# One of four head pairs of the first batch moved from TensorE transposes in float32 to DMA transposes of float16 halves

## The chip, the cores and the metric

The kernel runs on one core of one Trainium2 chip. The metric is the time of one execution on the device in microseconds (us). Three runs of the kernel before lie between 962.21 and 963.56 us, with a median of 963.2 us.

## The reference, cut to what matters

Two batches of attention with 8 heads, 768 tokens and head size 64 are followed by two dense stages on all 1536 tokens. A query sees only the keys of its own cluster.

```python
def _attn_ref(q, k, v, centroids):
    # q_assign, k_assign: argmax over 16 clusters of the normalized products
    mask = q_assign[:, :, :, None] == k_assign[:, :, None, :]
    scores = scale * np.matmul(q, k.transpose(0, 1, 3, 2))
    scores = np.where(mask, scores, -1000000000.0)
    scores = scores - np.max(scores, axis=-1, keepdims=True)
    attn = np.exp(scores)
    attn = attn / (np.sum(attn, axis=-1, keepdims=True) + 1e-09)
    return np.matmul(attn, v).astype(np.float32)

def _moe_ref(x, w_in, w_out):            # 512 -> 2048 -> 512
    h = x @ w_in
    g = h * np.clip(h + 3.0, 0.0, 6.0) / 6.0
    return (g @ w_out).astype(np.float32)

def _moe2_ref(x, domain_probs, w1, w2):  # 4 experts, 512 -> 1024 -> 512
    p = domain_probs / (domain_probs.sum(-1, keepdims=True) + 1e-09)
    for e in range(4):
        out += p[:, e:e + 1] * (np.maximum(x @ w1[e], 0.0) @ w2[e])
    return out.astype(np.float32)
```

The dense stages run as products of float16 halves: a number is a high half plus a low half, and three of the four products are taken.

## The kernel before, in words

**Stages.** The attention of batch 0 comes first (some 150 us), then the dense stages of batch 0, into which the attention of batch 1 is woven, then the dense stages of batch 1.

**Attention.** Two heads make a pair, and there are four pairs. Three blocks of 256 queries make a pair's work, and each block has four units: two heads, 128 queries each. A unit is: the scores in PSUM by TensorE (`scores`, tile `pss`), the row maximum by VectorE (tile `ut`), the exponential by ScalarE (tile `e`, 128x768 float32), and two tiny VectorE steps that make the reciprocal of the row sum.

**Batch 0, `turned`.** GpSimd multiplies `e` by the reciprocal in place (L751). TensorE turns `e` in six 128x128 transposes of float32 (L763, tile `pst`, two halves of three). ScalarE (L770) or VectorE (L772) copies each half of 384 columns out of PSUM into `pt`; a list of five letters gives four of five copies to ScalarE. A block ends with twelve float32 products with the values (L779, tile `psv`), and ScalarE and VectorE split the sum into the halves `x1h` and `x1l` (L787, L788).

**Batch 1, `block`.** A unit's `e` becomes two float16 halves in the tile `p`: the high half by GpSimd or ScalarE, which multiply on the way (L873, L871), the low half by VectorE from `e` and the high half (L875). One DMA from SP's queue turns the whole tile (L812, 12 squares of 128x128). A block ends with 36 float16 products (L825), with the values in halves too (`vh`, `vl`, L733 and L734).

**Fillers.** The first dense stage's weights come as 64-bit numbers and are packed into float32 during the attention of batch 0 (`conv_w`). A step is one GpSimd row (L974) and three VectorE rows (L976, L978, L980) on 128x512. Four rows L902 and L899 split the weights into halves. When the x1 of all pairs for the first 384 tokens is there, TensorE starts on the first dense product (L993 to L995, tile `psg1`), four tiles of 12 products one after the other in one PSUM buffer, until the attention's PSUM buffers are given back.

**What sets the order.** Every instruction is recorded as a task with a priority, and `Order.plan` places them by a list scheduler with a table of costs: an engine takes the task that can start first, ties by priority. Tasks of GpSimd, and VectorE tasks marked `lk`, are never planned at the same time. The plan is fixed when the program is built; each engine then works through its own list in that order. The list `seq` gives the order of the twelve blocks of batch 0 (block 3*pair + i), and the numbers in `PAR` shift priorities.

Of the kernel before, what the change touches and what calls it, by code (L numbers as in the profile page):

```python
# [9 lines left out]
F32 = mybir.dt.float32  # L10
# [17 lines left out]
def _f32(u):  # L28
# [10 lines left out]
PAR = dict(  # L39
    thr=3060,  # L40
    off=0.0,
    wsl="DD",
    wx=-1.7848102153653658,
    wxs=1.64249681070015,
    wx0=43.52497423987616,
    wl=7.46084025153843,
    slack=0.05,
    nl=0.5,
    vre=2,
    nbv=12.87796141218993,  # L50
    nbr=18.542111538044182,
    xw=[4.0, 8.0],
    prl=60.0,
    q0=-100.0,
    q1=6.0,
    psc="ms",
    ql=6,
    ahead=2.5,
    wait=0,
    wait0=0.8,  # L60
    until=20.0,
    wgap=4,
    ta=33.746613078702275,
    tu=2.609752841226513,
    lead0=24.331100661201216,
    lead2=1.5253475332630761,
    vlead2=-8.583792241787163,
    lead1=2.038891508477018,
    vlead=-37.093258968816514,
    avp=-9.334810999175945,  # L70
    parts=3,
    avpa=-4.3000394462166165,
    kn='PPPPPD',
    kt='AAADA',
    kb='AAPD',
    gl=["DDDD", "DDDD"],
    mx=28.649235830032236,
    sp=15.01076876764054,
    spc=7.053784887436649,
    wse=dict(i="P", o="S", **{"1": "P", "2": "A"}),  # L80
    v0=42.0,
    lr=0.3,
    spm=1.5,
    pem=0.0,
    v1=-24.49398218583093,
    a_pool=dict(raw=2, vr=4, sc=1, so=1, cs=2, oh=3, sm=2, e=7, pt=5, tiny=11, stk=4),
    b_pool=dict(raw=2, vr=2, sc=1, so=1, cs=1, oh=1, sm=2, e=2, p=3, pt=3, vh=1, vl=1, tiny=11, stk=2),
    xbb=1,
    loa="VP",
    lob="VV",  # L90
    r64p=8.97904547225396,
    slow=1.1760075282760927,
    psx=3,
    dup=["PSSS", "P"],
# [17 lines left out]
    btail=7.42405243741263,
    bu0=40.446540415353034,
    bdu=26.208100345557234,
    bvl=-0.8085585893733991,
    bpr=6.32743258604082,
)


# [267 lines left out]
def body(ctx: ExitStack, tc: tile.TileContext, qk, vd, cent, w_in, w_out, probs, w1, w2, out):  # L387
    nc = tc.nc
    B, H, _, S = qk.shape
    D, C = 64, 16  # L390
    NP = H // 2
    NT = S // 128
# [15 lines left out]
    G = PAR  # L408
# [87 lines left out]
    wx = fixed([128, B, NC2, 2], F32, "wx")  # L496
# [10 lines left out]
    pt = fixed([128, NTOK // 128, E], F32, "pt")  # L507
    sp = fixed([128, NTOK // 128], F32, "sp")
# [65 lines left out]
    class Attn:  # L574
        def __init__(self, b, g, gp, n):
            self.b = b
            self.xb = PAR["xbb"]
# [146 lines left out]
        def values(self, hp, p):  # L724
            b, st = self.b, self.pair[hp]
            vr, inv, k = st["vr"], vm[:, b, 1:2], (vm, (b, 1))
            if b == 0:
                st["v"] = vr
                return
            vr = self.buf("vr", [128, 2, NT, D], F32)  # L730
            dma(393e3, max(p(0), self.seen + 0.1 * hp), lambda: nc.sync.dma_start(out=vr.t, in_=vd[b, hp]), [], [vr])
            vh, vl = self.buf("vh", [128, 2, NT, D], F16), self.buf("vl", [128, 2, NT, D], F16)
            act(S, p(2), lambda: nc.scalar.activation(out=vh.t, in_=vr.t, func=AF.Copy, scale=inv), [vr, k], [vh], ap=True)  # L733
            dve(S, p(2), lambda: nc.vector.scalar_tensor_tensor(  # L734
                out=vl.t, in0=vr.t, scalar=inv, in1=vh.t, op0=ALU.mult, op1=ALU.subtract), [vr, k, vh], [vl], ap=True, lk=True)
            st["v"] = (vh, vl)
# [54 lines left out]
        def block(self, hp, blk, p, kinds, xb, avp):  # L791

            b, st = self.b, self.pair[hp]
# [616 lines left out]
```

## Time and profile before

| | |
|---|---|
| Median of three runs | 963.2 us |
| The profiled execution | 964.7 us, span 962.9 us |
| Mean granted clock of TensorE | 0.993 of full speed |
| Busy, share of the span | PE 96%, DVE 76%, ACT 68%, POOL 37% |

Busy time is how long at least one instruction of the engine ran. PE is TensorE, DVE is VectorE, ACT is ScalarE, POOL is GpSimd and SP is the engine whose queue issues the DMAs. The shares are means over stages with different limits, so the change is read from the stage in which it lies: the attention of batch 0, from the first scores at about 13 us to the last of its blocks at about 148 us.

### The profile page before, as it was taken

The numbers are of one execution on the slowest core, as the hardware profiler recorded it, in microseconds if no ns is written. First come the engines' busy times: TensorE is split into PE (matmuls) and PEld (weight loads), VectorE is DVE, ScalarE is ACT, GpSimd is POOL, SyncE is SP. The second block draws the span as 40 slices with busy tenths as digits, with TensorE's granted clock in tenths as the row PEclk, the third lists the DMA queues.
The fourth block names the chain that finished last, engine by engine and source line by source line (L and its number), as shares of the span: only waits on it lengthen the run. The fifth ranks groups of instructions, "written<-read, shape, count | busy, mean of one in ns | idle before, by whom it ended". The sixth has DMA issues, their size and how long they took to land.

```text
span 962.9 us, 16168 instructions
## 1 busy us (share of the span) xinstructions
PE 922.3 (96%) x5633; PEld 546.9 (57%) x5633; DVE 727.3 (76%) x1513; ACT 658.4 (68%) x1372; POOL 356.8 (37%) x394
## 2 busy tenths in 40 slices
PE   5899999999989999999999999999999999999998
PEld 3577775555655565555565555666655555555553
DVE  8898785887779898799788986965578665554543
ACT  6899996767687796988788754566458654555411
POOL 3465744234533435736355321001132442434100
PEclk9999999999999999999999999999999999999999
DMA  7534339786526484586457587432021221212001
GB/s 235 142 89 116 127 106 328 237 288 206 175 93 188 90 174 104 127 179 132 120 107 182 152 159 191 144 109 90 21 67 66 88 70 63 88 45 87 1 1 66
DMA packets 124369, 121.63 MB, mean 126 GB/s; under 512 B 81472, under 2 KB 81472, under 8 KB 124288
## 3 DMA queue, kind: packets, MB, share of 16 engines
q1 hardware_dynamic: 124288, 120.61, 44.3%
q8 instruction: 44, 0.72, 0.3%
q14 instruction: 37, 0.30, 0.1%
HBM read 81.32 MB, written 14.68 MB: 100 GB/s over the span
## 4 chain that ended last, share of the span: by engine, by line
PE 44%; DVE 4%; ACT 3%; DMA 1%; POOL 1%; issue 1%; SPq 1%; POOLq 0%; ACTq 0%
PE psm L993 6%; PE psm L994 6%; PE psm L995 6%; PE psw L1070 6%; PE psw L1072 5%; PE psw L1071 5%; PE psg L995 2%; PE psg L993 2%; PE psg L994 2%; DMA wraw<-in_w 1%; PE psv L825 1%; PE pss L843 1%; ACT e L852 1%; PE pss L845 1%; DMA pt<-p 1%
## 5 line engine op out<-in xcount | busy, mean ns | idle before, releaser
L899 POOL TENSOR_TENSOR w<-wraw,w 128x512 f16<-128x512 f32 (+1 forms) x128 | 135.1, 1075 | 174.5 <-ACT w L898 132.1
L993 PE MATMUL psm<-w,h 128*128 128x512 f16 x384 | 146.3, 381 | 2.6 <-DVE h L1233 2.5
L995 PE MATMUL psm<-w,h 128*128 128x512 f16 x384 | 146.0, 380 | 0.1
L994 PE MATMUL psm<-w,h 128*128 128x512 f16 x384 | 146.0, 380 | 0.0
L851 DVE TENSOR_REDUCE ut<-pss 128x1 f32<-128x768 f32 x96 | 91.0, 951 | 16.8 <-PE pss L845 15.8
L852 ACT ACTIVATE e<-pss,ut 128x768 f32<-128x768 f32 x96 | 86.1, 898 | 18.0 <-DVE ut L851 15.3
L897 POOL TENSOR_SCALAR wraw<-wraw,wsc 128x512 f32<-128x512 f32 x64 | 45.8, 724 | 124.0 <-DMA wraw<-in_w 43.0
L1080 ACT ACTIVATE keep<-psw 128x384 f32<-128x384 f32 x96 | 46.7, 486 | 63.9 <-PE psw L1072 63.8
L898 ACT ACTIVATE w<-wraw 128x512 f16<-128x512 f32 (+1 forms) x128 | 72.4, 582 | 20.2 <-POOL wraw L897 11.1
L994 PE MATMUL psg<-g,w 128*128 128x384 f16 x256 | 83.4, 326 | 1.2 <-DVE g L1143 1.2
L993 PE MATMUL psg<-g,w 128*128 128x384 f16 x256 | 83.6, 327 | 1.0 <-DVE t L1141 0.6
L995 PE MATMUL psg<-g,w 128*128 128x384 f16 x256 | 83.6, 326 | 0.0
L1257 DVE SCALAR_TENSOR_TENSOR oa<-psm,pq,oa 128x512 f32<-128x512 f32 x84 | 61.9, 745 | 23.1 <-PE psm L995 23.1
L994 PEld LDWEIGHTS <-w 128*128 128x128 f16 x512 | 50.3, 98 | 39.0 <-issue 8.1
L995 PEld LDWEIGHTS <-w 128*128 128x128 f16 x512 | 50.2, 98 | 35.9 <-issue 3.3
L993 PEld LDWEIGHTS <-w 128*128 128x128 f16 x512 | 50.9, 99 | 33.4 <-issue 1.7
L843 PE MATMUL pss<-ka,qa 128*128 128x384 f32 x192 | 60.8, 398 | 8.1 <-ACT e L852 7.7
L1233 DVE SCALAR_TENSOR_TENSOR h<-psw,h 128x384 f16<-128x384 f32 x78 | 43.1, 553 | 29.0 <-ACT h L1232 28.8
L995 PEld LDWEIGHTS <-h 128*128 128x128 f16 x384 | 37.7, 98 | 46.1 <-DVE h L1233 0.6
L1070 PE MATMUL psw<-tx,ws 128*128 128x384 f16 x192 | 62.7, 327 | 0.9 <-ACT keep L1080 0.7
L1071 PE MATMUL psw<-tx,ws 128*128 128x384 f16 x192 | 62.6, 326 | 0.3 <-DVE tx L1022 0.3
L993 PEld LDWEIGHTS <-h 128*128 128x128 f16 x384 | 38.5, 100 | 42.5 <-issue 5.4
(199 smaller groups left out, 2402.6 us busy)
## 6 DMA issues: line engine op xcount, KB each, us to landing
wraw<-in_w SPq DMA_DIRECT2D x128, 256.0 KB, 3.4
r<-in_w_in SPq DMA_DIRECT2D x16, 512.0 KB, 4.6
r<-in_w_out SPq DMA_DIRECT2D x16, 512.0 KB, 3.9
w<-hl_i SPq DMA_DIRECT2D x32, 256.0 KB, 3.2
w<-hl_o SPq DMA_DIRECT2D x32, 256.0 KB, 3.9
raw<-in_qk SPq DMA_DIRECT2D x16, 384.0 KB, 4.3
vr<-in_vd SPq DMA_DIRECT2D x12, 384.0 KB, 4.9
hl_i<-w SPq DMA_DIRECT2D x16, 256.0 KB, 3.0
```

What stands on the lines that cost most here:

```text
L843: nc.tensor.matmul(ps[:, f, 0:HS], qa[:, qs], ka[:, f * HS:f * HS + HS], start=True, stop=False)
L851: dve(S, p, lambda: nc.vector.tensor_reduce(out=nb(), in_=ps[:, :, 0:HS], axis=AX.XY, op=ALU.max, negate=True), [ps], [(tb, n)])
L852: act(S, p, lambda: nc.scalar.activation(out=e.t.rearrange("p (a b) -> p a b", a=2), in_=ps[:, :, 0:HS], func=AF.Exp, bias=nb(), scale=1.0 ...
L898: act(c, p, lambda w=w, raw=raw, c=c: nc.scalar.activation(out=w[:, 0, 0:c], in_=raw[:, 0:c], func=AF.Copy), [raw], [(w, 0)])
L899: pool(c, p, lambda w=w, raw=raw, c=c: nc.gpsimd.tensor_tensor(out=w[:, 1, 0:c], in0=raw[:, 0:c], in1=w[:, 0, 0:c], op=ALU.subtract), [raw ...
L993: nc.tensor.matmul(o_, ah, bh, start=i == 0, stop=False)
L994: nc.tensor.matmul(o_, ah, bl, start=False, stop=False)
L995: nc.tensor.matmul(o_, al, bh, start=False, stop=i == 3)
L1070: nc.tensor.matmul(o_, ah, bh, start=not more and k == 0, stop=False, skip_group_check=more)
L1071: nc.tensor.matmul(o_, ah, bl, start=False, stop=False, skip_group_check=more)
L1072: nc.tensor.matmul(o_, al, bh, start=False, stop=k == 1, skip_group_check=more)
L1257: dve(512, p, lambda: nc.vector.scalar_tensor_tensor(out=oa[:, t], in0=ps.t, scalar=q, in1=oa[:, t], op0=ALU.mult, op1=ALU.add), [ps, qk], ...
```

## The change

Pair 2 of batch 0 (`ct0=(2,)`) goes through `block` in place of `turned`, with the letters `DDDD`: GpSimd makes the high half of each unit, VectorE the low half. The pair's values are split into `vh` and `vl` once. The blocks of pair 2 (6, 7, 8) alternate with those of pair 3 (9, 10, 11) in `seq`; before they stood 6, 7, 9, 10, 8, 11. Three tiles `p` and one each of `vh` and `vl` are added to batch 0's buffers. Many priorities in `PAR` have new values.

```diff
+    ct0=(2,),
+    kc="DDDD",
+    avc=-5.0,
+    vc=0.0,
...
-    seq=[0, 1, 3, 2, 5, 4, 6, 7, 9, 10, 8, 11],
+    seq=[0, 1, 3, 2, 5, 4, 9, 6, 10, 7, 11, 8],
...
-            if b == 0:
+            if b == 0 and hp not in G["ct0"]:
                 st["v"] = vr
                 return
-            vr = self.buf("vr", [128, 2, NT, D], F32)
-            dma(393e3, max(p(0), self.seen + 0.1 * hp), lambda: nc.sync.dma_start(out=vr.t, in_=vd[b, hp]), [], [vr])
+            if b:
+                vr = self.buf("vr", [128, 2, NT, D], F32)
+                dma(393e3, max(p(0), self.seen + 0.1 * hp), lambda: nc.sync.dma_start(out=vr.t, in_=vd[b, hp]), [], [vr])
...
-            col = XSC / (VSC * PSC)
+            col = XSC / (VSC * PSC) if b else 1.0 / PSC
...
         for blk in range(NBQ):
-            a0.turned(hp, blk, lambda i, t0=when[hp, blk]: t0 + i * T_UNIT, G["avpa"])
+            if hp in G["ct0"]:
+                a0.block(hp, blk, lambda i, t0=when[hp, blk]: t0 + i * T_UNIT, G["kc"], 1, G["avc"])
+            else:
+                a0.turned(hp, blk, lambda i, t0=when[hp, blk]: t0 + i * T_UNIT, G["avpa"])
```

In the changed kernel the same lines stand 4 or 5 lines further down (L763 is L768, L875 is L880, L978 is L983).

The first place is VectorE's list near the end of the attention of batch 0. `ut` is the row maximum or its tiny steps, `wconv` the weights that are packed, `pt` a turned half, `t` and `g` the first dense product's result, `x1l` a finished block. Before:

```order
L851 TENSOR_REDUCE ut_1869<-pss_1850 128x1
L772 COPY pt_1844<-pst_1865 128x384
L860 TENSOR_SCALAR ut_1831<-ut_1831 128x1
L980 SCALAR_TENSOR_TENSOR wconv_1669<-r64_1299,wconv_1669 128x512
L861 RECIPROCAL ut_1831<-ut_1831 128x1
L860 TENSOR_SCALAR ut_1869<-ut_1869 128x1
L978 SCALAR_TENSOR_TENSOR wconv_1823<-r64_1774,wconv_1823 128x512
L861 RECIPROCAL ut_1869<-ut_1869 128x1
L980 SCALAR_TENSOR_TENSOR wconv_1823<-r64_1774,wconv_1823 128x512
L1141 SCALAR_TENSOR_TENSOR t_1908<-t_1908,psg1_1835 128x384
L772 COPY pt_1894<-pst_1925 128x384
L788 SCALAR_TENSOR_TENSOR x1l0_611<-psv_1891,vm_66,x1h0_594 128x256
```

And now, at the same place (`p` is the tile of halves, L880 the low half):

```order
L983 SCALAR_TENSOR_TENSOR wconv_1887<-r64_1836,wconv_1887 128x512
L880 SCALAR_TENSOR_TENSOR p_1928<-e_1900,ut_1878,p_1928 128x768
L793 SCALAR_TENSOR_TENSOR x1l0_619<-psv_1909,vm_66,x1h0_611 128x256
L856 TENSOR_REDUCE ut_1962<-pss_1939 128x1
L880 SCALAR_TENSOR_TENSOR p_1956<-e_1907,ut_1893,p_1956 128x768
L865 TENSOR_SCALAR ut_1962<-ut_1962 128x1
L1148 TENSOR_TENSOR g_1937<-t_1916,g_1937 128x384
L866 RECIPROCAL ut_1962<-ut_1962 128x1
L1146 SCALAR_TENSOR_TENSOR t_1971<-t_1971,psg1_1948 128x384
L985 SCALAR_TENSOR_TENSOR wconv_1887<-r64_1836,wconv_1887 128x512
L880 SCALAR_TENSOR_TENSOR p_1979<-e_1968,ut_1962,p_1979 128x768
L1148 TENSOR_TENSOR g_1981<-t_1971,g_1981 128x384
```

The steps of the packing stand among the attention's steps as before; the copies out of PSUM have gone for pair 2, and a low half stands there for each of its units, the last one (p_1979) four rows ahead of the end of the attention's own work.

The second place is the end of TensorE's share of that attention: the last scores (`pss`), what stands between, and the last products with the values (`psv`). Before:

```order
L843 MATMUL pss_1850<-ka_1096,qa_1089 128x384 x2
L845 MATMUL pss_1850<-kb_1162,qb_1120 128x384 x2
L763 MATMUL pst_1859<-ident_60,e_1772 128x128 x3
L763 MATMUL pst_1865<-ident_60,e_1772 128x128 x3
...
L995 MATMUL psg1_1990<-x1h0_594,w_1593 128x384
L779 MATMUL psv_2009<-pt_1894,vr_316 64x256
```

And now:

```order
L848 MATMUL pss_1939<-ka_1182,qa_1168 128x384 x2
L850 MATMUL pss_1939<-kb_1191,qb_1188 128x384 x2
L998 LDWEIGHTS w_1429
L998 MATMUL psg1_1948<-x1h0_611,w_1429 128x384
...
L1000 MATMUL psg1_2010<-x1h0_611,w_1464 128x384
L830 LDWEIGHTS vh_567
L830 MATMUL psv_2020<-pt_1881,vh_567 64x256
```

Between the last scores and the last products with the values there now stand 30 products of the first dense stage (two and a half tiles `psg1`) and no transposes; 12 products of it stand ahead of the last scores and 6 behind the products with the values. Before, 33 of those 48 stood ahead of the last products with the values and 15 behind.

The third place is SP's list. Where loads of 64-bit weights (`r64`) stood one after the other, the DMA transposes now stand among them:

```order
L817 DMA_TRANSPOSE pt_1627<-p_1579 128x12x128
L975 DMA r64_1653<-in_w_in 128x1024
L817 DMA_TRANSPOSE pt_1627<-p_1638 128x12x128
L975 DMA r64_1704<-in_w_out 128x1024
L817 DMA_TRANSPOSE pt_1710<-p_1684 128x12x128
L817 DMA_TRANSPOSE pt_1710<-p_1708 128x12x128
L975 DMA r64_1757<-in_w_out 128x1024
```

Twelve transposes are added; a load behind one is issued only after the transpose has been, and that waits for its low half.

## Rows read from the trace of the kernel before

**Rows 1.** Busy time by stretch: from:to, us; PE, PEld, DVE, ACT, POOL; clock, DMA

```profile
13.00:80.00 67.00, 58.53 (x397) 42.94 (x394) 61.97 (x136) 59.23 (x124) 34.26 (x37) 0.95 0.50 141
80.00:148.60 68.60, 64.27 (x473) 49.33 (x473) 55.62 (x137) 61.45 (x140) 41.10 (x47) 1.00 0.38 119
153.00:300.00 147.00, 141.63 (x853) 83.05 (x851) 111.91 (x226) 109.61 (x228) 61.22 (x74) 0.99 0.64 217
```

**Rows 2.** Timeline of VectorE: start us, us, then the instruction; sixth block's end

```profile
79.91 0.48 DVE L788 SCALAR_TENSOR_TENSOR x1l<-psv,vm,x1h 128x256 f16<-128x256 f32 x1
```

**Rows 3.** Timeline of TensorE: a block's products with the values, a unit's transposes

```profile
46.01 2.81 PE L779 MATMUL psv<-pt,vr 128*64 128x256 f32 x24
48.75 0.88 PE L763 MATMUL pst<-ident,e 128*128 128x128 f32 x6
...
50.16 0.82 PE L763 MATMUL pst<-ident,e 128*128 128x128 f32 x6
50.74 0.60 PE L843 MATMUL pss<-ka,qa 128*128 128x384 f32 x2
```

**Rows 4.** Timeline of TensorE: a block of batch 1 and what follows it

```profile
335.92 0.85 PE L825 MATMUL psv<-pt,vh 128*64 128x256 f16 x12
...
338.01 0.39 PE L993 MATMUL psm<-w,h 128*128 128x512 f16 x1
```

**Rows 5.** Groups of instructions by form, 80 to 148.6 us: count, busy us, mean ns, idle

```profile
L751 POOL TENSOR_SCALAR e<-e,ut 128x768 f32<-128x768 f32 x26 | 23.9, 926 | 19.6 <-PE pst L763 6.7 <-DVE ut L861 3.8 <-ACT e L852 2.9
...
L770 ACT ACTIVATE pt<-pst 128x384 f32<-128x384 f32 x44 | 20.1, 494 | 1.7 <-PE pst L763 1.3
...
L772 DVE COPY pt<-pst 128x384 f32<-128x384 f32 x11 | 6.1, 551 | 2.5 <-PE pst L763 2.5
L978 DVE SCALAR_TENSOR_TENSOR wconv<-r,wconv 128x512 int32<-128x512 int32 x8 | 5.7, 715 | 0.1
...
L980 DVE SCALAR_TENSOR_TENSOR wconv<-r,wconv 128x512 int32<-128x512 int32 x8 | 5.5, 684 | 0.0
...
L976 DVE TENSOR_SCALAR wconv<-wconv 128x512 int32<-128x512 int32 x7 | 3.1, 444 | 0.8 <-POOL wconv L974 0.8
...
L902 DVE SCALAR_TENSOR_TENSOR w<-wconv,wsc,w 128x512 f16<-128x512 f32 x4 | 2.9, 745 | 0.0
...
L1143 DVE TENSOR_TENSOR g<-t,g 128x384 f16<-128x384 f32 x2 | 1.1, 550 | 0.0
...
L675 DVE TENSOR_TENSOR oh<-cs,mx 128x384 bf16<-128x384 f32 x1 | 0.9, 924 | 0.0
```

**Rows 6.** Instructions on tile p in batch 1: duration ns min/median/max; DMA landing

```profile
L875 DVE SCALAR_TENSOR_TENSOR p<-e,ut,p x36: 1000/1011/1602, 317.3 to 590.2; 128x768 f16<-128x768 f32 x36
...
L873 POOL TENSOR_SCALAR p<-e,ut x12: 899/906/912, 329.4 to 589.2; 128x768 f16<-128x768 f32 x12
...
DMA to landing us min/median/max: 3.6/4.0/6.7
```

**Rows 7.** Instructions of line 976, duration ns min/median/max

```profile
L976 DVE TENSOR_SCALAR wconv<-wconv x32: 401/422/1376, 28.4 to 235.7; 128x512 int32<-128x512 int32 x32
```

**Rows 8.** Busy time by stretch, two dense ones

```profile
80.00:90.00 10.00, 8.93 (x62) 6.67 (x63) 8.93 (x23) 8.58 (x21) 8.91 (x8) 1.00 0.26 62
...
24.00:36.00 12.00, 9.65 (x60) 7.10 (x59) 11.97 (x36) 9.05 (x20) 6.37 (x8) 0.86 0.60 156
```

**Rows 9.** Timeline of VectorE, the two rows on two inputs before 90 us

```profile
87.02 0.93 DVE L978 SCALAR_TENSOR_TENSOR wconv<-r,wconv 128x512 int32<-128x512 int32 x1
...
89.39 0.92 DVE L675 TENSOR_TENSOR oh<-cs,mx 128x384 bf16<-128x384 f32 x1
```

**Rows 10.** Timeline of TensorE, the end of the attention of batch 0

```profile
147.82 0.33 PE L995 MATMUL psg<-x1h,w 128*128 128x384 f16 x1
149.98 0.32 PE L993 MATMUL psg<-x1h,w 128*128 128x384 f16 x1 [1.84 <-DVE t L1141]
...
151.76 0.33 PE L995 MATMUL psg<-x1h,w 128*128 128x384 f16 x1
```

More of the change, by code (lines that the diff above doesn't have):

```diff
@@ L42 @@
     wsl="DD",
-    wx=-1.7848102153653658,
+    wx=-2.2504429911643062,
     wxs=1.64249681070015,
-    wx0=43.52497423987616,
-    wl=7.46084025153843,
+    wx0=43.50730777874564,
+    wl=7.364647491268241,
     slack=0.05,
@@ L49 @@
     vre=2,
-    nbv=12.87796141218993,
-    nbr=18.542111538044182,
+    nbv=12.84003995968822,
+    nbr=17.879757093734796,
     xw=[4.0, 8.0],
+    ct0=(2,),
+    kc="DDDD",
+    avc=-5.0,
+    vc=0.0,
     prl=60.0,
     q0=-100.0,
-    q1=6.0,
+    q1=7.169479564805545,
     psc="ms",
@@ L60 @@
     wait0=0.8,
-    until=20.0,
+    until=20.474484084238878,
     wgap=4,
[L63 to L70, printed above, removed]
+    ta=33.82429798049329,
+    tu=2.6054164164858413,
+    lead0=24.38941968821655,
+    lead2=1.5696374598142093,
+    vlead2=-16.23868846141527,
+    lead1=2.1498286844841727,
+    vlead=-4.820577093532606,
+    avp=-5.926955675381867,
     parts=3,
-    avpa=-4.3000394462166165,
-    kn='PPPPPD',
+    avpa=-4.2100322989173975,
+    kn='PPPPPP',
     kt='AAADA',
@@ L76 @@
     gl=["DDDD", "DDDD"],
-    mx=28.649235830032236,
-    sp=15.01076876764054,
-    spc=7.053784887436649,
+    mx=28.42957232445986,
+    sp=15.706444076444198,
+    spc=9.340045527570249,
     wse=dict(i="P", o="S", **{"1": "P", "2": "A"}),
-    v0=42.0,
+    v0=42.50032448502036,
     lr=0.3,
@@ L84 @@
     pem=0.0,
-    v1=-24.49398218583093,
-    a_pool=dict(raw=2, vr=4, sc=1, so=1, cs=2, oh=3, sm=2, e=7, pt=5, tiny=11, stk=4),
+    v1=-26.859076459892776,
+    a_pool=dict(raw=2, vr=4, sc=1, so=1, cs=2, oh=3, sm=2, e=7, pt=5, tiny=11, stk=4, p=3, vh=1, vl=1),
     b_pool=dict(raw=2, vr=2, sc=1, so=1, cs=1, oh=1, sm=2, e=2, p=3, pt=3, vh=1, vl=1, tiny=11, stk=2),
@@ L90 @@
     lob="VV",
-    r64p=8.97904547225396,
-    slow=1.1760075282760927,
+    r64p=4.367580803347444,
+    slow=1.1711405140056712,
     psx=3,
@@ L95 @@
     dpx=2,
-    trp=5.076571153367599,
+    trp=4.880737426751388,
     trh=2,
     parta=6,
-    cv0=131.77161799616468,
-    cvd=14.831817816757964,
+    cv0=131.96049987990045,
+    cvd=15.071608329127226,
     cva=2,
@@ L110 @@
     two=[0, 0],
-    seq=[0, 1, 3, 2, 5, 4, 6, 7, 9, 10, 8, 11],
[L112 to L116, printed above, removed]
+    seq=[0, 1, 3, 2, 5, 4, 9, 6, 10, 7, 11, 8],
+    btail=7.367867965850532,
+    bu0=40.04659757051773,
+    bdu=25.833110530721868,
+    bvl=-5.20583503779102,
+    bpr=6.223014872498889,
 )
@@ L576, in __init__ @@
             self.b = b
-            self.xb = PAR["xbb"]
+            self.xb = PAR["xbb"] if b else 1
             prep = ("raw", "sc", "so", "cs", "oh", "sm") + (("vr",) if b else ())
@@ L1276, in body @@
         a0.prep(hp, lead, G["loa"] if hp else "VV")
-        a0.values(hp, (lambda x, t0=t0: t0 - G["vlead"] - G["vlead2"] * hp + x) if hp else (lambda x: 3.0 + x))
+        a0.values(hp, (lambda x, t0=t0: t0 + G["vc"] + x) if hp in G["ct0"] else lambda x: 0.0)
         for blk in range(NBQ):
-            a0.turned(hp, blk, lambda i, t0=when[hp, blk]: t0 + i * T_UNIT, G["avpa"])
+            if hp in G["ct0"]:
+                a0.block(hp, blk, lambda i, t0=when[hp, blk]: t0 + i * T_UNIT, G["kc"], 1, G["avc"])
+            else:
+                a0.turned(hp, blk, lambda i, t0=when[hp, blk]: t0 + i * T_UNIT, G["avpa"])
     for i in range(2 * NC1):
```

## The prediction, made before the changed kernel ran

> **What bounds the kernel now.** I read the stretches of the attention of batch 0 first. Up to 80 us TensorE, VectorE and ScalarE are all busy for 58 to 62 of 67 us; from 80 to 148.6 us TensorE leads with 64.27 of 68.60, ScalarE has 61.45 and VectorE 55.62 [rows 1]. The cut at 80 lies at the end of the sixth of the twelve blocks (79.91 us [rows 2]); pairs 2 and 3, where the change lies, are behind it. Taken engine by engine, TensorE bounds that second half and VectorE has 13 us to spare. After 153 us TensorE is busy for 141.63 of 147 us [rows 1], so what the second half gains or loses is carried on nearly whole.
>
> There is a limit that no engine's row shows by itself. I next read, per line, how an instruction's longest duration compares with its median. L976, a VectorE row on one tile in SBUF, has a median of 422 ns and a longest of 1376 [rows 7]: the difference, 954 ns, is just one GpSimd row L751 (926 [rows 5]). The low half of batch 1 goes from 1011 to 1602 [rows 6]. So these VectorE rows and GpSimd's take turns, and their times must be added. VectorE's reads of PSUM (the maximum, the copies, the split of a block) are not counted here. From 80 to 148.6 us GpSimd is busy for 41.10 us [rows 1], and the VectorE rows that work from SBUF come to 5.7 + 5.5 + 3.1 + 2.9 + 1.1 + 0.9 = 19.2 us [rows 5]. Together 60.3 us in 68.6, a pace of 0.88. This turn-taking pair is nearly as full as TensorE.
>
> **The change, part by part.** *TensorE loses 9.0 us.* A unit's six transposes take 50.74 - 50.16 = 0.58 us, twelve units 7.0 us [rows 3]. A block's products with the values took 48.75 - 46.01 = 2.74 us [rows 3] and take 338.01 - 335.92 = 2.09 us in halves [rows 4]: 0.65 for each of three blocks, 2.0 us.
>
> *ScalarE loses 8 us or more.* Of pair 2's 24 copies out of PSUM four of five are ScalarE's: 19 of 494 ns, 9.4 us; VectorE loses five of 551, 2.8 us [rows 5]. One split of the values is added to each.
>
> *GpSimd is unchanged.* A high half (906 ns [rows 6]) stands for a scaling in place (926 [rows 5]), and its list up to the last of them has as many rows, fillers too.
>
> *VectorE gets twelve low halves*, 12 x 1.011 = 12.1 us [rows 6], all of the kind that takes turns. The split of the values is one more of the same form, early in the first half, where I cost it at nothing since 61.97 of 67 us leave a gap [rows 1]; without that cover it is 1.0 us.
>
> *The reordering* moves one packing step's two long rows (1.4 us) and the one-hot (0.9) out of the second half ahead of 80 us, and one row on q, of the low half's form and taken at its 1.0, into it: -1.3 us.
>
> The sum for the pair that takes turns, from the sixth block to the last low half, is 60.3 + 12.1 - 1.3 = 71.1 us. That last low half is in VectorE's list behind all of them. At a pace of 1.00 it ends at 80.0 + 71.1 = 151.1 us. Then come, one after the other, the DMA transpose (4.0 us to landing [rows 6]), the products with the values (2.1 [rows 4]) and the last 6 of the 48 products that the first dense stage can do in its one PSUM buffer (0.16 each by the step of the rows, 1.0 [rows 10]): 158.2 us. Before, the last of these 48 starts at 151.76 and ends its step at 151.9 [rows 10]. The loss is 6.3 us. TensorE's spare work does not help: two and a half tiles of that stage stand between the last scores and those products, and beyond them it has only what waits for the pair's x1.
>
> Something comes back: after 153 us TensorE idles for 5.4 of 147 us [rows 1], and a packing that is no later than before while the stage starts later shortens such waits; I take 1.0 of it, bounds 0 and 2. Net +5.3 us.
>
> **The pace** is the unknown. No row shows the pair at its limit for long, so I bound it. From 80 to 90 us GpSimd has 8.91 us [rows 8], and VectorE's rows of the kind 0.93 and the first 0.6 of 0.92 [rows 9]: 1.05, above one because the recorded ends overlap the next start and hold waiting. At 1.05 the loss is 80 + 67.7 + 7.1 - 151.9 = 2.9; at 0.95 the 71.1 us become 74.8 and the loss 10.0; at the 0.88 of now 80.8 and 16.0. I take 1.00, nearest to the dense row, since TensorE and ScalarE, which held the pace down, each get some 9 us lighter.
>
> The Trainium skill ("SBUF — State Buffer", section "SBUF: two separate sides") calls this an exclusive lock on a port pair that VectorE and GpSimd share, held for the whole instruction, and counts a VectorE instruction with two SBUF inputs among the holders; the low half is one. By that rule no pace over 1.00 exists and the floor of the loss would be 6.3; the rows reach 1.05, so my low end stays 2.9.
>
> The profiled execution took 964.7 us for a span of 962.9, 1.5 over the median; I put the difference on the median: 963.2 + 5.3 = 968.5 us. With the paces 0.95 to 1.05 and what comes back, this case's own range is 965 to 972.
>
> **Rivals.** *TensorE's relief goes through.* If the pair that takes turns keeps up (low halves slip in where VectorE now idles for 13 us), the second half shortens by TensorE's 9.0 us, less one more wait for the single PSUM buffer, 1.84 us [rows 10], since now two tile ends instead of one lie bare: -7.2 us, 956 us. For it: TensorE is the busiest engine, and only recorded durations, not waits of TensorE, speak for the pair. Against it: it asks the pair for 71 us of turns in 61.
>
> *VectorE alone is the bound*, and GpSimd runs beside it: its 55.62 us get 12.1 - 2.8 - 1.3 more, 63.6 us, which at the 11.97 of 12 us of its densest row [rows 8] take 63.8 and end at 143.8; with the tail of 7.1 this is 150.9, 1.0 earlier: 962.2 us, and with a little idle time no change. Against it are the 1376 and 1602 ns of [rows 6, 7].
>
> *SP's queue stalls the pair.* A transpose waits for its low half in SP's list, and the weight loads behind it start late; the packing row that waits for them holds VectorE's list, and with it the next maximum. This decides once the loads land after their place in that list; then the pace stays at the 0.88 of now: +16.0, 979 us. For it: loads and transposes alternate there. Against it: the DMAs are busy only 0.38 of that stretch [rows 1].
>
> That the change does not do what it says is excluded: the order holds the twelve transposes and the transposes on TensorE are 72 fewer.
>
> **How the numbers follow.** My forecast, the pair that takes turns at a pace near one, gets 0.56; the relief going through 0.19; VectorE alone 0.12; the stalled queue 0.13. A difference of 0.2% (1.9 us, 961.3 to 965.1) is about what a measurement of this kernel can tell from no change. Faster: the relief and a fifth of VectorE alone, 0.21. Same: the rest of VectorE alone near its dense pace and the low end of my case, 0.10. Slower: 0.69. The range from 959 to 977 leaves out most of the relief case and the far end of the stalled queue.
>
> **What would show it.** Right: the last products with the values start 5 us or more after a TensorE idle time released by the DMA into `pt`; VectorE and GpSimd together have about 71 us of turns between the sixth block and the last low half; TensorE's busy share of that stretch falls to some 55 of 71 us; low halves over 1.3 us. Wrong: the sixth block ends elsewhere than at 80 us, or the 48th product of the first dense stage ends before 152 us; then the pair was not the limit. A lower granted clock in that stretch (it was 0.95 up to 80 us, where TensorE idles more, and 1.00 after [rows 1]) would add to the loss beyond this sum.

## The result, and the profile after

| kernel | median, us | ratio to the kernel before | profiled execution, us | its span, us |
|---|---|---|---|---|
| before | 963.4 | 1 | 964.7 | 962.9 |
| changed | 978.2 | 1.0129 [1.0088, 1.0169] | 978.9 | 977.1 |

The change makes the kernel slower: by 1.3% as the ratio on record has it, by 1.5% between the two medians (14.8 us) and between the two profiled executions (14.2 us). Slower was forecast, at 968.5 us. A loss of 5.3 us was expected; the measured median lies outside the case's own range of 965 to 972 and just outside the wide range of 959 to 977.

One thing on record has to be put right first. The x1l row at 79.91 us of [rows 2] ends the fifth of the twelve blocks, not the sixth as the text ahead says. The stretch that was summed is the right one; only its name is wrong. Below it is called "from the fifth block to the last x1l".

This is the first stretch of [rows 1] in the changed kernel (length; then busy us and instructions of TensorE, its weight load, VectorE, ScalarE, GpSimd; granted clock, DMA share, GB/s):

```profile
13.00:80.00 67.00, 57.12 (x361) 41.63 (x359) 60.62 (x129) 56.26 (x120) 32.71 (x35) 0.92 0.49 146
```

TensorE has 57.1 us of 67 where it had over 58, at a clock of 0.92 where it was 0.95. So the loss begins ahead of the pair's first unit. The block that ended at 79.91 + 0.48 us now ends at 86.9, the last one at 167.6 instead of 148.6:

```profile
86.44 0.47 DVE L793 SCALAR_TENSOR_TENSOR x1l<-psv,vm,x1h 128x256 f16<-128x256 f32 x1
167.16 0.42 DVE L839 SCALAR_TENSOR_TENSOR x1l<-psv,x1h 128x256 f16<-128x256 f32 x1 [4.00 <-ACT x1h L838]
```

The span's difference of 14.2 us falls into three parts: 86.9 - 80.4 = 6.5 up to the fifth block, 80.7 - 68.2 = 12.5 from there to the last x1l, and -4.8 after it (977.1 - 167.6 = 809.5 us against 962.9 - 148.6 = 814.3).

The stretch from the fifth block to the last x1l, of the kernel before and then of the changed one, in the columns of the window above:

```profile
80.40:148.60 68.20, 63.87 (x471) 48.97 (x470) 55.22 (x136) 61.05 (x139) 40.70 (x47) 1.00 0.38 118
```
```profile
86.90:167.60 80.70, 64.19 (x443) 47.85 (x442) 67.44 (x144) 55.68 (x121) 38.40 (x45) 0.89 0.62 165
```

Read the VectorE column against the length. VectorE's busy time grows by 67.4 - 55.2 = 12.2 us, and the stretch by 12.5. The time in which VectorE stands idle is 13.0 us before and 13.3 after, but these are not the same waits. The changed kernel's stretch in three parts, cut at the seventh block and at the last low half:

```profile
86.91:108.33 21.42, 19.46 (x134) 14.75 (x133) 15.67 (x42) 19.21 (x41) 16.62 (x19) 1.00 0.32 95
108.33:159.07 50.74, 38.97 (x263) 29.36 (x262) 48.11 (x99) 34.28 (x75) 21.77 (x27) 0.87 0.70 182
159.07:167.58 8.51, 5.73 (x48) 3.72 (x48) 3.64 (x8) 2.19 (x5) 0.00 (x0) 0.80 0.87 241
```

In the long middle part, where the pair's low halves stand, VectorE is idle for only 2.6 of 50.7 us; in the tail behind the last low half it is idle for 4.9 of 8.5, 4.0 of them waiting for the last block. Before, it idled for 5.5 us up to the seventh block and for 7.4 from there on, with no such tail. That the two sums agree is chance.

ScalarE has 5.4 us less to do, GpSimd 2.3; TensorE has 28 matmuls fewer in the records and takes as long for them, at a clock of 0.89 instead of 1.00. Where the 12.2 us come from, by line (busy, mean ns of one, idle before them), first before and then after:

```profile
L978 DVE SCALAR_TENSOR_TENSOR wconv<-r,wconv 128x512 int32<-128x512 int32 x8 | 5.7, 715 | 0.1
L980 DVE SCALAR_TENSOR_TENSOR wconv<-r,wconv 128x512 int32<-128x512 int32 x8 | 5.5, 684 | 0.0
L772 DVE COPY pt<-pst 128x384 f32<-128x384 f32 x11 | 6.1, 551 | 2.5 <-PE pst L763 2.5
```
```profile
L880 DVE SCALAR_TENSOR_TENSOR p<-e,ut,p 128x768 f16<-128x768 f32 x12 | 12.4, 1044 | 1.0 <-POOL p L878 1.0
L983 DVE SCALAR_TENSOR_TENSOR wconv<-r,wconv 128x512 int32<-128x512 int32 x8 | 7.2, 897 | 0.0
L985 DVE SCALAR_TENSOR_TENSOR wconv<-r,wconv 128x512 int32<-128x512 int32 x8 | 6.3, 786 | 0.0
L777 DVE COPY pt<-pst 128x384 f32<-128x384 f32 x6 | 3.3, 547 | 0.2 <-PE pst L768 0.2
```

The low halves add 12.4 us, the copies lose 2.8, and the sixteen packing rows, the same in number, take 2.3 us more, since more of them wait for a GpSimd row inside their recorded time (the longest, with the GpSimd row beside it, below); one more maximum adds 0.9. That is 12.8; smaller rows give 0.6 back. VectorE hardly waits for the pair's own chain: the low halves wait for their high halves for 1.0 us in all.

```profile
129.63 0.91 POOL L878 TENSOR_SCALAR p<-e,ut 128x768 f16<-128x768 f32 x1 [3.61 <-DVE ut L865]
129.74 1.32 DVE L983 SCALAR_TENSOR_TENSOR wconv<-r,wconv 128x512 int32<-128x512 int32 x1
```

The end of the stretch is the chain forecast, with one more link. In the order of time: SP's transposes, the first of six products of the dense stage that had waited for VectorE's row on `t`, and TensorE's last products with the values:

```profile
153.31 7.18 SPq L817 DMA_TRANSPOSE pt<-p  x3
```
```profile
161.85 0.33 PE L998 MATMUL psg<-x1h,w 128*128 128x384 f16 x1 [2.78 <-DVE t L1146]
163.71 1.49 PE L830 MATMUL psv<-pt,vh 128*64 128x256 f16 x12
165.00 1.04 PE L830 MATMUL psv<-pt,vl 128*64 128x256 f16 x12
165.88 0.82 PE L830 MATMUL psv<-pt,vh 128*64 128x256 f16 x12
```

The last low half ends at 159.07 us; transpose and wait take 4.6 us (4.0 forecast), the products 3.0 (2.1 forecast; the clock is 0.83 from 160 to 170 us), six more products of the dense stage 0.9. The last transpose was issued at 159.10 and landed 3.2 us later, at 162.3. The remaining 1.4 us of the wait are the six dense products ahead in TensorE's list; TensorE had idled for VectorE's `t`, not for the DMA.

### The profile page after: what moved, and what is told of

Same layout as the page of the kernel before. It is cut to its first block, busy times and chain, and to the rows that moved or that the text cites. A ratio compares the mean times of both kernels' runs of the same rounds, so it can differ in the third digit from the quotient of the medians.

```text
span 977.1 us, 16121 instructions
## 1 busy us (share of the span) xinstructions
PE 923.3 (94%) x5597; PEld 546.3 (56%) x5597; DVE 741.8 (76%) x1521; ACT 652.7 (67%) x1354; POOL 354.9 (36%) x394
## 4 chain that ended last, share of the span: by engine, by line
PE 45%; DVE 6%; ACT 2%; DMA 2%; issue 1%; POOL 1%; SPq 0%; ACTq 0%; POOLq 0%
PE psm L998 6%; PE psm L999 6%; PE psm L1000 6%; PE psw L1075 6%; PE psw L1076 6%; PE psw L1077 6%; PE psg L998 2%; PE psg L1000 2%; PE psg L999 2%; DMA wraw<-in_w 1%; PE psv L830 1%; PE pss L848 1%; DVE ws L960 1%; PE pss L850 1%; DVE p L880 1%
## 5 line engine op out<-in xcount | busy, mean ns | idle before, releaser
L1262 DVE SCALAR_TENSOR_TENSOR oa<-psm,pq,oa 128x512 f32<-128x512 f32 x84 | 61.7, 743 | 22.4 <-PE psm L1000 22.3
L999 PEld LDWEIGHTS <-w 128*128 128x128 f16 x512 | 50.3, 98 | 43.1 <-issue 12.7
L1000 PEld LDWEIGHTS <-h 128*128 128x128 f16 x384 | 37.5, 98 | 45.9 <-DVE h L1238 0.7
L1075 PE MATMUL psw<-tx,ws 128*128 128x384 f16 x192 | 62.7, 327 | 0.5 <-ACT keep L1085 0.5
L1076 PE MATMUL psw<-tx,ws 128*128 128x384 f16 x192 | 62.6, 326 | 0.1
L1077 PE MATMUL psw<-tx,ws 128*128 128x384 f16 x192 | 62.6, 326 | 0.0
```

The costliest lines, as they stand in the source:

```text
L999: nc.tensor.matmul(o_, ah, bl, start=False, stop=False)
L1000: nc.tensor.matmul(o_, al, bh, start=False, stop=i == 3)
L1075: nc.tensor.matmul(o_, ah, bh, start=not more and k == 0, stop=False, skip_group_check=more)
L1076: nc.tensor.matmul(o_, ah, bl, start=False, stop=False, skip_group_check=more)
L1077: nc.tensor.matmul(o_, al, bh, start=False, stop=k == 1, skip_group_check=more)
L1262: dve(512, p, lambda: nc.vector.scalar_tensor_tensor(out=oa[:, t], in0=ps.t, scalar=q, in1=oa[:, t], op0=ALU.mult, op1=ALU.add), [ps, qk], ...
```

## The experiments

Three theories were held against each other. *Turns*, as forecast: GpSimd's rows and VectorE's rows on SBUF exclude each other and their sum is the limit. *VectorE alone*: its list, in order, is the limit. *Numbers*: the new numbers of the table and the new order of blocks cost the time, not the pair's work. In each kernel I read the stretch from the fifth block to the last x1l as above. Its part from the fifth to the seventh block took 21.3 to 21.4 us in six kernels whose edits hardly touch it, so differences under half a microsecond are not read. Each stretch is read from one profiled execution. The kernel before ran beside each of three sets, with medians of 963.4, 965.9 and 964.9 us; ratios are to the one of the same set.

**Low half, high half, maximum.** Three edits with the order of the changed kernel kept row for row.

```
-  out=pp[:, j, 1], in0=e.t, in1=pp[:, j, 0]                       (VectorE, 768 columns)
+  out=f(pp[:, j, 1]), in0=e[:, 0:HS], in1=f(pp[:, j, 0])          (384 columns)
```

> The changed kernel with the same planned order; the subtraction that makes the low half of the probabilities in the first batch covers 384 instead of 768 columns (half of its result is left out). Twelve subtractions of 1.044 us become some 0.6 us: VectorE has 5 us less, and GpSimd and VectorE together too. Turns (the two engines exclude each other on SBUF): the end of the first batch's 48th first-expert product comes 5 us earlier, 162.6 instead of 167.6, total 973. VectorE alone: also 5 us earlier, total 973. GpSimd's late first high half decides: at most 1 us, total 977 to 978.

```
-  nc.gpsimd.tensor_scalar(out=pp[:, j, 0], in0=e.t, ...)          (GpSimd, 768 columns)
+  nc.gpsimd.tensor_scalar(out=f(pp[:, j, 0]), in0=e[:, 0:HS], ...)
```

> The changed kernel with the same planned order; GpSimd's scaling that makes the high half covers 384 instead of 768 columns (half of its result is left out). Twelve scalings of 0.904 us become some 0.47 us: GpSimd has 5.2 us less, VectorE's own instructions stay. Turns: 48th product 5 us earlier, total 973. VectorE alone: less than 1 us, total 977 to 978. GpSimd's queue decides in 90 to 104 us: 1 to 2 us, total 976 to 977.

```
-  tensor_reduce(out=nb(), in_=ps[:, :, 0:HS], op=ALU.max)
+  tensor_reduce(out=nb(), in_=ps[:, :, 0:HS // 2], op=ALU.max)    (float16 pair's units)
```

> The changed kernel with the same planned order; in the float16 pair's twelve units the maximum reads 384 of the 768 scores, out of PSUM (the other half of the scores is left out of the maximum). Twelve instructions of 0.948 us become some 0.55 us: VectorE has 4.8 us less, and none of it on SBUF. Turns: 0 to 1 us, total 977 to 978. VectorE alone: 4.8 us, total 973.4.

Measured: 974.2 us, 1.0108 [1.0083, 1.0134]; 975.7, 1.0127 [1.0111, 1.0142]; 975.9, 1.0132 [1.0113, 1.0151]. The ratios overlap one another and that of the changed kernel, 1.0129 [1.0088, 1.0169]; the stretch of each tells more:

```profile
85.70:161.50 75.80, 61.68 (x443) 46.07 (x442) 62.47 (x144) 55.15 (x121) 38.94 (x45) 0.93 0.65 168
```
```profile
87.10:165.90 78.80, 64.52 (x443) 48.32 (x442) 66.11 (x144) 55.34 (x121) 34.63 (x45) 0.89 0.65 170
```
```profile
85.00:164.40 79.40, 64.19 (x443) 48.05 (x442) 63.77 (x144) 55.13 (x121) 39.66 (x45) 0.89 0.62 168
```

The low half gives 4.9 us, as both turns and VectorE alone have it. The high half takes 3.8 us from GpSimd and gives 1.9: turns wanted 5, VectorE alone under 1; VectorE's own recorded time is 1.3 us shorter too, as its rows wait less for GpSimd inside their recorded time. The maximum takes 3.7 us from VectorE and gives 1.3: VectorE alone wanted 4.8, turns 0 to 1. Neither theory holds by itself. In the third kernel VectorE's idle time grew by 2.3 us, among it the low half's wait for the high half, 2.1 us where the changed kernel has 1.0:

```profile
DVE p L881 <- POOL p L879: 2.1, 4, 0.8
```

**High half and maximum together.** If the wait for GpSimd ate what the maximum gave, the two edits together should give more than their sum.

```
   both edits of the second and third kernel above
```

> The changed kernel with the same planned order and both of two earlier edits: GpSimd's twelve high halves cover 384 of 768 columns, and the float16 pair's twelve maxima read 384 of 768 scores (the other halves are left out). Apart they shortened the stretch from the fifth block's end to the last x1l by 1.9 and 1.3 us while they took 3.8 us from GpSimd and 3.7 us from VectorE. VectorE's list with the waits for the high halves close behind it: together they give more than the sum, 4.5 to 6 us of the stretch, total 972 to 973. Independent costs: 3.2 us, 975. A third limit (TensorE at its lower clock, ScalarE): 2 us or less.

Measured: 974.3 us, 1.0104 [1.0079, 1.013]; the stretch 76.7 us, 4.0 less than in the changed kernel. This is above the sum (3.2) and below the bound set for the theory (4.5): it leans to the wait and does not show it.

**The high half on ScalarE.** The strongest test of the turns, with nothing left out.

```
-  nc.gpsimd.tensor_scalar(out=pp[:, j, 0], in0=e.t, scalar1=rs(), ...)
+  nc.scalar.activation(out=pp[:, j, 0], in_=e.t, func=AF.Copy, scale=rs())
```

> The changed kernel with the same planned order; ScalarE instead of GpSimd makes the twelve high halves in the first batch (nothing left out). GpSimd loses 12 x 0.904 = 10.8 us, ScalarE gains about 11 us and has 25 us to spare between the fifth block and the last x1l; VectorE's own rows stay. Turns: the stretch shortens by 8 us or more, total 968 to 970. VectorE's list in order, with the waits for the lock and for the high halves: 2 to 4 us, total 974 to 976. If ScalarE's list becomes the wait: no gain, 978 or more.

Measured: 978.7 us, 1.0127 [1.0102, 1.0152].

```profile
85.20:165.90 80.70, 67.31 (x443) 50.36 (x442) 65.97 (x143) 64.95 (x133) 28.47 (x33) 0.85 0.60 161
```

GpSimd has 9.9 us less to do and the stretch is as long as before, to the tenth. The lock is there: the row L983 falls from a mean of 897 to 758 ns, and VectorE's busy time by 1.5 us. But what it sets free goes into waits (VectorE stands idle for 14.7 instead of 13.3 us), as ScalarE now has the high halves in its list ahead of exponentials. So the sum of the turns is not what holds this kernel's stretch. This run alone doesn't settle it for the changed kernel: the expectation had named ScalarE's list as a possible new wait. ScalarE is busy for 9.3 us more, the clock is 0.85, and the equal length is a sum of a part up to the seventh block that is 1.4 us longer, a middle that is 0.4 shorter and a tail that is 1.0 shorter. That a ScalarE with more to spare would have passed more of it on is not excluded.

**Packing at half width, in the changed kernel and, as a control, in the kernel before.** These rows are VectorE's, and no chain of the scores passes through them.

```
-  out=a(), in0=r[:, :, 0], scalar=29, in1=a(), ...
+  out=a()[:, 0:256], in0=r[:, 0:256, 0], scalar=29, in1=a()[:, 0:256], ...   (all three rows of a packing step)
```

> The changed kernel with the same planned order; the three VectorE rows that pack a chunk of a double into a float (one tensor_scalar, two scalar_tensor_tensor) work on 256 of 512 columns (the other half of the weights is left unpacked). From the fifth block's end to the last x1l these are 24 rows, about 5.4 us of VectorE, and none of them is on a chain of the scores. VectorE's list in order: the stretch of 80.7 us shortens by 5 to 6 us, and with the first half's rows the total is 970 to 972. Turns: the same 5, they are rows on SBUF. A chain through the pair's own units (maximum, exponential, high half, low half): at most 2 us, total 976 to 978.

> The kernel before with the same edit (256 of 512 columns packed, half of the weights left unpacked): the control. If TensorE bounds the second half there, as its 64.3 of 68.6 us say: 0 to 1 us, total 962 to 963.5. If VectorE's list or the turns are as tight there as in the changed kernel: 5 us or more, total 958 or less.

Measured: 970.5 us, 1.0046 [1.0028, 1.0065]; the control 961.0, 0.9953 [0.9931, 0.9976]. The changed kernel's stretch, then that of the control:

```profile
85.90:160.60 74.70, 62.59 (x443) 47.09 (x442) 62.00 (x144) 55.03 (x121) 37.80 (x45) 0.91 0.67 168
```
```profile
80.20:148.00 67.80, 63.82 (x472) 49.12 (x470) 50.67 (x138) 61.04 (x139) 40.24 (x47) 1.00 0.40 124
```

The same relief of VectorE, 5.4 and 4.5 us, shortens the stretch by 6.0 us in the changed kernel and by 0.4 in the kernel before, where TensorE keeps its 63.8 us and VectorE only idles for longer, 17.1 instead of 13.0. Of the 6.0 us, 3.6 fall between the seventh block and the last low half, where VectorE has 4.7 us less, and 2.3 in the tail, whose clock is 1.00 where it was 0.80. This is the clearest result: before the change VectorE's list does not bound the stretch, and after it that list does. That TensorE bounds it before is read from its 63.8 of 67.8 us; no run relieved TensorE alone. Outside the stretch the control gained more than expected, about 2 us by the spans (961.0 us in the median where 962 to 963.5 were expected); the packing weighs on later stages too.

**The numbers and the order of blocks.** Three kernels undo one part of the change each: no pair in float16 with the new numbers; the pair with the old numbers; the pair with the new numbers and the old order of blocks.

```
-  ct0=(2,),
+  ct0=(),
```

> The changed kernel with every new number of the table, but no pair in float16 (the set of such pairs empty): all four pairs as in the kernel before, planned with the new numbers and the new interleaved order of blocks. If the whole loss is the pair's own work: 963, as the kernel before. If the new numbers cost the 6.5 us by which the fifth block's end is late in the changed kernel (86.44 against 79.91 us): 969 to 970. If the interleaved order costs more than that: up to 978.

```
   every number of the table as before, and ct0=(2,), kc="DDDD", avc=-5.0, vc=0.0, the pools p, vh, vl
```

> The pair in float16 as in the changed kernel, but with every number of the table that the kernel before has (order of blocks 0 1 3 2 5 4 6 7 9 10 8 11, leads, due times). The changed kernel without the pair took 966.1, so the pair itself costs 12 us and the new numbers 2.7. If the two add up: 963.4 + 12 = 975.4, and the fifth block ends near 80 us as before. If the new order is what makes the pair bearable: over 980. If the pair's loss is mostly the new order's: under 970.

```
-  seq=[0, 1, 3, 2, 5, 4, 9, 6, 10, 7, 11, 8],
+  seq=[0, 1, 3, 2, 5, 4, 6, 7, 9, 10, 8, 11],
```

> The changed kernel with its own numbers, but the order of blocks of the kernel before (0 1 3 2 5 4 6 7 9 10 8 11): pair 2's first blocks are not interleaved with the fourth pair's. The planned order then has 15 packing rows of VectorE instead of 24 between the fifth block and the last x1l, and the others behind it. If the stretch alone counts: 9 rows of 0.7 us less, 972. If VectorE's packing must be paid at either place: the stretch shortens by 6 us or more, the total by less than 3, 975 to 978. If the interleaving was what helps: over 980.

Measured: 966.1 us, 1.0032 [1.0020, 1.0044]; 977.6, 1.0114 [1.0087, 1.0140]; 974.7, 1.0109 [1.0074, 1.0144]. So the new numbers cost about 3 us by themselves, and the pair most of the rest, whichever numbers stand beside it (977.6 with the old ones, where 975.4 was expected if the two costs added up). The third kernel shows that the packing is paid at one place or the other: with 15 packing rows in its stretch instead of 24 it reaches the last x1l at 153.6 us, 14 us earlier than the changed kernel, and ends only 6.8 us earlier in its profiled execution (970.3 us of span), 3.5 us by the medians. The fifth block ends late in all three, at 84.2, 85.3 and 85.2 us; with the old numbers it was expected near 80.

**Numbers chosen anew, with the pair and without.** The pair's version makes half of the high halves on ScalarE, has the order of blocks 1 0 3 2 5 4 9 10 6 7 11 8, and its packing due later.

```
-  kc="DDDD", r64p=4.37, spc=9.34, avp=-5.93, seq=[0, 1, 3, 2, 5, 4, 9, 6, 10, 7, 11, 8],
+  kc="AADD", r64p=-9.52, spc=-0.22, avp=-26.52, seq=[1, 0, 3, 2, 5, 4, 9, 10, 6, 7, 11, 8],
...
```

> Nothing left out: pair 2 in float16 with ScalarE making the high halves of every first two of four units and GpSimd the others, and the numbers of the table chosen anew (packing due later, order of blocks 1 0 3 2 5 4 9 10 6 7 11 8). If the pair's work on VectorE costs its 12 us wherever it stands: 970 or more. If the loss of the changed kernel is one of place in the lists: 960 to 964, level with the kernel before or better.

> Nothing left out: all four pairs as in the kernel before, with numbers of the table chosen anew in the same way as for the pair's version, the control for it. New numbers alone: 958 to 961. If the pair is worth having, its version is below this one; if only the numbers matter, this one is at least as fast.

Measured: 966.4 us, 1.0015 [0.9993, 1.0036], with the pair; 962.6, 0.9977 [0.9964, 0.9991], without. Both are some 2 us above what was expected (960 to 964, and 958 to 961). The stretch of each:

```profile
83.90:149.70 65.80, 55.35 (x432) 41.09 (x432) 61.04 (x137) 54.59 (x116) 31.20 (x37) 1.00 0.69 167
```
```profile
81.80:147.70 65.90, 63.00 (x462) 47.63 (x461) 55.79 (x136) 59.86 (x137) 39.77 (x46) 1.00 0.38 120
```

With the pair VectorE is now busy for 61.0 of 65.8 us, and TensorE has 10 us to spare at full clock: TensorE's relief is there, 8.5 of the 9.0 us forecast, and VectorE's list is what is left. It is 6.4 us shorter in this stretch than in the changed kernel, since two packing steps and two maxima stand elsewhere. From 110 to 150 us it leaves 1.3 us idle, while GpSimd has 12.8 of 40; with VectorE's 24.5 us of rows on SBUF that is 37.4 of turns, less than VectorE's own list:

```profile
110.00:150.00 40.00, 32.22 (x269) 22.79 (x269) 38.66 (x79) 31.31 (x66) 12.82 (x15) 1.00 0.92 226
```

So some 11 us of the changed kernel's loss (1.0129 against 1.0015 of the kernel before; 13.5 us between the two spans) can be had back with the pair in place; the pair then equals the kernel before within what can be measured. The version without the pair is faster than the kernel before by a quarter of a per cent and than the pair's version by 0.4%, so the pair itself costs some 4 us against a control made with the same care. How much of the 11 us comes from where the rows stand in the lists, how much from the high halves on ScalarE, and which of the new numbers did it, was not tried one by one.

Side by side, the stretch from the fifth block to the last x1l (us; idle is the length less VectorE's busy time):

| kernel | length | VectorE busy | VectorE idle | GpSimd busy | clock |
|---|---|---|---|---|---|
| before | 68.2 | 55.2 | 13.0 | 40.7 | 1.00 |
| before, packing halved | 67.8 | 50.7 | 17.1 | 40.2 | 1.00 |
| changed | 80.7 | 67.4 | 13.3 | 38.4 | 0.89 |
| low half halved | 75.8 | 62.5 | 13.3 | 38.9 | 0.93 |
| high half halved | 78.8 | 66.1 | 12.7 | 34.6 | 0.89 |
| maximum halved | 79.4 | 63.8 | 15.6 | 39.7 | 0.89 |
| both of these | 76.7 | 62.6 | 14.1 | 35.0 | 0.91 |
| high half on ScalarE | 80.7 | 66.0 | 14.7 | 28.5 | 0.85 |
| packing halved | 74.7 | 62.0 | 12.7 | 37.8 | 0.91 |
| pair, new numbers again | 65.8 | 61.0 | 4.8 | 31.2 | 1.00 |
| no pair, new numbers again | 65.9 | 55.8 | 10.1 | 39.8 | 1.00 |

And the part of it from the seventh block to the last low half, where the pair's rows stand (us; turns are GpSimd's busy time and that of VectorE's rows on SBUF, added; in brackets the share of the length):

| kernel | length | VectorE busy | turns | from there to the last x1l |
|---|---|---|---|---|
| changed | 50.7 | 48.1 (0.95) | 50.1 (0.99) | 8.5 |
| low half halved | 47.5 | 43.9 (0.92) | 45.5 (0.96) | 6.9 |
| high half halved | 48.9 | 46.8 (0.96) | 45.7 (0.94) | 8.5 |
| maximum halved | 49.6 | 45.8 (0.92) | 52.0 (1.05) | 8.5 |
| both of these | 47.1 | 44.6 (0.95) | 46.8 (0.99) | 8.3 |
| high half on ScalarE | 50.4 | 46.2 (0.92) | 37.9 (0.75) | 7.5 |
| packing halved | 47.1 | 43.4 (0.92) | 44.6 (0.95) | 6.2 |
| pair, new numbers again | 38.5 | 38.0 (0.99) | 35.2 (0.91) | 7.6 |

In all eight VectorE is busy for 0.92 to 0.99 of this part, while the turns go from 0.75 to 1.05 of it. A pace above one can stand there because a VectorE row's recorded time holds its wait for GpSimd, so the two are counted twice. The list of VectorE, with 0.5 to 4 us of waits in it, is the account that holds for all of them; the turns fail where the high half goes to ScalarE.

## Why the prediction was right in sign and short in size

*What bounds the kernel before.* TensorE fits: the control, with 4.5 us less on VectorE, left its 63.8 us and nearly the whole length as they were. Wrong for the second limit: GpSimd's and VectorE's turns were taken for nearly as full as TensorE, and the same control took 4.5 us out of them for a gain of 0.4.

*The turns, 71.1 us at a pace of 1.00.* Measured from the fifth block's end at 86.9 to the last low half at 159.07: 72.2 us. GpSimd's 38.4 and the 31.2 of VectorE's SBUF rows in it make 69.6, a pace of 0.96. The term came out within 1.1 us, and that is in part luck: with 9.9 us fewer of GpSimd's rows the stretch stayed at 80.7 us, so the sum does not set the length by itself. What it held correctly is the growth of VectorE's list, 12.1 forecast for the low halves and 12.4 measured. Packing rows longer by 2.3 us, waiting for GpSimd, were what the records show of the lock here. The reading that led to the turns had the wrong partner: the row of 1376 ns [rows 7] stands at 195 us, in the dense stage, beside a GpSimd row L899 of 1.16 us, not beside an L751. That the two take turns stands.

```profile
195.04 1.16 POOL L899 TENSOR_TENSOR w<-wconv,w 128x512 f16<-128x512 f32 x1
195.10 1.38 DVE L976 TENSOR_SCALAR wconv<-wconv 128x512 int32<-128x512 int32 x1 [0.18 <-POOL wconv L974]
```

The Trainium skill ("SBUF — State Buffer", section "SBUF: two separate sides") has the lock right, and the rows of L983 agree (897 ns with GpSimd's high halves, 758 without them); that a lock exists does not make it the limit.

*VectorE alone* was the rival nearest to the mechanism. Its busy time came out as forecast, 63.8 us from the fifth block to the last low half (63.6 forecast). Its price of 962 us was wrong, since it let VectorE run at the pace of its densest row from the start: 8.4 us of idle time stand in that list, 5.7 of them ahead of the seventh block, where the part is nearly as full of TensorE as before (19.5 of 21.4 us, 22.3 of 24.2 before). It too began at 80.0 us. In the middle part VectorE did reach a share of 0.95, so the forecast's "TensorE and ScalarE, which held the pace down, each get some 9 us lighter" fits there and not ahead of it.

*The step that failed* is the start. The sum began at 80.0 us, the end of the fifth block as it was, and took the stretch ahead of it for unchanged; it ends 6.9 us later than that. The text had named this as what would prove it wrong. Beside it stand +1.1 for the turns and +1.4 for the tail (8.5 instead of 7.1, the products at a lower clock), and -0.5 since 1.5 us and not 1.0 came back: 5.3 + 6.9 + 1.1 + 1.4 - 0.5 = 14.2.

Of the other signs, the last products with the values did not start behind a wait for the DMA, as the tail above shows. The low halves took 1.04 us in the mean, and one of twelve was over 1.3. The turns made 69.6 of the 71 us, and TensorE was busy for 58.4 of 72.2 us where 55 of 71 had been named. So the direction was right, the size was off mainly by the start, and the runs support VectorE's list as the limit and not the turns.

Why the fifth block is late is settled only in part. The split of the pair's values, taken at nothing, is the first new row in the lists of ScalarE and VectorE, at 36 and 38 us, but no delay is left of it at the third block (61.0 us, 61.7 before); the fourth block is 2.9 us late and the fifth 6.5. One piece is the clock, which the forecast had named as a loss outside its sum: TensorE waits 1.9 us for a GpSimd row, and the fourth block's products, at the lower clock, take 4.50 us where the third block's took 2.81. The stretch is at 0.67 of the clock now and was at 1.00 before:

```profile
56.81 2.81 PE L784 MATMUL psv<-pt,vr 128*64 128x256 f32 x24
68.16 0.88 PE L768 MATMUL pst<-ident,e 128*128 128x128 f32 x6 [1.93 <-POOL e L756]
69.68 4.50 PE L784 MATMUL psv<-pt,vr 128*64 128x256 f32 x24
70.00:75.00 5.00, 5.00 (x34) 2.97 (x34) 4.06 (x9) 2.63 (x6) 2.16 (x4) 0.67 0.12 23
```
```profile
70.00:75.00 5.00, 5.00 (x46) 3.89 (x43) 4.73 (x7) 4.51 (x11) 2.46 (x3) 1.00 0.21 38
```

That is 1.7 us. The place also scatters: six kernels, the changed one among them, have the same lists up to the fifth block, and it ended at 86.7 to 87.1 us in the three whose clock had fallen from 40 to 46 us as well (0.72), at 85.0 to 85.7 in the three whose clock had not. So the start came between 5.0 and 7.1 us late, and 6.9 is near the upper end.

Without the pair the new numbers alone put the fifth block at 84.2 us (and 2.5 us on the span); with the pair and the old numbers it is at 85.3; together 86.9. So each goes with a delay; whether they add up can't be told from one trace each with such a scatter. The pair's list counts fewer units done there. VectorE's maxima (one for a unit) by window, before and after:

```profile
60.00:90.00 30.00, 12.36 (x13) 1.00 0.42 108
```
```profile
60.00:90.00 30.00, 9.32 (x10) 0.94 0.45 128
```

The lists part from those of the kernel before between 36 and 44 us, and no single row is shown to cause the rest; TensorE waits longest there for copies out of PSUM, 3.6 us between 36 and 90 against 1.8 before:

```profile
PE pst L768 <- ACT pt L775: 3.6, 4, 2.2
```
```profile
PE pst L763 <- ACT pt L770: 1.8, 2, 1.3
```

*SP's queue* had nearly the right time, 979 us, by luck, and not its mechanism: the weight loads hold ScalarE up for 0.9 us and the transposes TensorE for 1.1 us between 104 and 168 us, and VectorE's list waits for no DMA there at all.

```profile
ACT wconv L978 <- DMA r<-in_w_out: 0.9, 1, 0.9
PE psv L830 <- DMA pt<-p: 1.1, 1, 1.1
```

*TensorE's relief goes through* was wrong for this kernel and half right for the idea: in the version with new numbers TensorE's time in the stretch is 55.35 us instead of 63.87, but the length follows VectorE's list.

## What to carry to other kernels

When work leaves the engine that bounds a stretch, look for the engine whose list receives any of it, and set its new busy time as the floor: 55.62 + 12.1 - 2.8 - 1.3 = 63.6 us of VectorE up to the last low half was at hand before the change, and 63.8 was measured. Then add its idle time part by part, not as one number. Ahead of the pair's rows it stayed (5.5 us before, 5.7 after), beside them 2.6 us were left of it, and behind the last of them came a tail of 8.5 us in which the list waits. That VectorE's idle time as a whole is 13 us both before and after is chance; the version with new numbers has 4.8. And where a planner rebuilds the lists, no stretch ahead of the change counts as unchanged: read the new order from the start, or keep a margin of several us for it.

## What the runs showed of the hardware

The granted clock followed TensorE's waiting, but not by its amount alone. In the changed kernel it fell to the lower of its two levels (0.50, 1.2 of 2.4 GHz) behind a slice in which TensorE was busy for 1.66 of 3 us, and was whole again from 118 us on:

```profile
106.00:109.00 3.00, 2.77 (x20) 1.84 (x16) 2.72 (x6) 1.82 (x5) 1.32 (x2) 1.00 0.44 100
109.00:112.00 3.00, 1.66 (x6) 1.53 (x7) 2.89 (x9) 2.70 (x6) 1.74 (x4) 0.81 0.96 214
112.00:115.00 3.00, 1.77 (x7) 1.26 (x7) 2.61 (x4) 2.92 (x7) 1.96 (x3) 0.50 1.07 261
115.00:118.00 3.00, 3.00 (x15) 2.90 (x14) 2.95 (x8) 1.45 (x3) 1.51 (x2) 0.56 0.95 242
118.00:121.00 3.00, 1.95 (x26) 1.50 (x26) 2.92 (x7) 1.75 (x5) 1.71 (x3) 1.00 0.83 307
```

In the pair's version with new numbers a slice with still less, 1.12 of 3 us, left it whole:

```profile
121.00:124.00 3.00, 1.12 (x7) 0.80 (x6) 2.87 (x7) 2.51 (x5) 2.40 (x3) 1.00 1.09 254
```

Executions of the same lists differ too: from 40 to 46 us the clock was 0.72 in three of the six kernels named above and 1.00 in the others.

At the lower clock TensorE's matmuls took longer: a transpose 305 ns in the mean of the stretch where it was 276 before, and the stretch's 443 matmuls 64.2 us where 471 had taken 63.9. As VectorE was nearly always busy meanwhile, how much of the 12.5 us the clock adds through longer chains was not separated; in the tail, 8.5 us at 0.80 stand beside 6.2 and 6.9 us at 1.00 in two of the kernels above.
